# Top-k attention with a mixture of experts: shorter chains at five pairs of heads, six pairs' masks on another engine, and the first expert stage regrouped

## The chip, the cores and the metric

The kernel runs on one core of one Trainium2 chip. The metric is the device time of one execution in microseconds (us), the median of several runs.

## The reference, cut to what matters

```python
# q, k, v: (2, 8, 576, 64)
scores = matmul(q, k.T) / 8
kth    = 32nd largest of each row of 576 scores
scores = where(scores >= kth, scores, -1e9)
attn   = exp(scores - max); attn = attn / (sum(attn) + 1e-9)
x      = matmul(attn, v)                       # as (1152, 512), heads side by side
p      = probs / (sum(probs) + 1e-9)           # 4 experts
x      = sum over e of p[:, e] * (relu(x @ w1[e]) @ w2[e])        # 512 -> 1024 -> 512
h      = max(x @ m1, x @ m2, x @ m3); out = h @ m_out              # 512 -> 768 -> 512
```

The last four matrices come in as float64 and are made float32 on the chip.

## The kernel before, in words

**Attention** is cut into 36 pairs, numbered 1 to 36 here: 128 rows (one of nine tiles) of two heads. Each pair takes eight slots of an order written out in `attention()`; in a slot, every step that was put there with `at_slot` or `two` is emitted on its engine. The dictionaries `FIRST`, `TIGHT` and `LOOSE` say how many slots after the pair's first each step stands. Per head, DVE (VectorE) finds the 32 largest of 576 scores with four MAX8 (L434) and three MATCH_REPLACE8 (L436). Then the mask: a multiply by a comparison on DVE (L462, which also sums), or a comparison (L465) and a multiply (L466) on POOL (GpSimd) with the sum on ACT (L470), or three operations on ACT (ScalarE; L455 to L457, which also sum and take the exponent). `ON_POOL` and `ON_ACT` list by number from 0 which pair's head takes which. Then come transposes `psp` (L480, L485) and their copies `pt` (L483, L488), the guard on the sums `rs` (L493), the reciprocal (L499), its spread and transpose (`rb`, `psr`, `r`), the product with v `psv` (L522, L525), and the norm (L532), in which DVE multiplies `psv` by `r` and writes `x`. `split_x` makes a high and a low part of `x` for later matmuls.

**The experts** follow the tiles in stages. Stage 0 (tile 0 alone, `first_alone`, matmuls L751 and L766) and the stage of one other single tile (L788, L829) use unsplit float32 weights, called `whole`; the other stages use high and low parts of weights (`whi`, `wlo`, L268 and L274) and three matmuls for each product (L667 to L669). In stage 0 one expert's first layer came after the other's: e outside, the four 128-wide pieces a of the model dimension inside.

**The order of the expert work** is set while the program is built. `products()` is a generator of expert matmuls; after each slot the main loop advances it until its running count of PE time reaches a goal that grows by DVE's estimated time in that slot. If the next matmul's `x` is not made yet, what is left of that goal is dropped. So a piece of `x` that is made some slots earlier lets expert matmuls stand earlier in PE's queue. `x_ready` takes a pair's `x` once its slot `last` has passed; for the third pair of a tile, `READY` slots more.

**Weights** are loaded by SP's DMA queue: `raw` pieces, split on ACT and POOL, at most `W_AHEAD` (4) pieces ahead of use; `whole` pieces straight into the buffers of the split parts. The last 12 pieces of the program are of the final maximum over three products (`largest`), whose weights are converted from float64 in the slots from 306 on (`to_float32`).

**The end**: after pair 36 only expert and final matmuls are left. ACT copies each output tile out of PSUM (L947) and issues its DMA (L948).

Of the kernel before, what the change touches and what calls it, by code (L numbers as in the profile page):

```python
# [20 lines left out]
BEGIN, READY = 4, 4  # L21
# [17 lines left out]
FIRST = dict(stag=2, new=1, scores=-12, trans=11, pv=17, rec=16, lag=2, sum=4)  # L39
TIGHT = dict(stag=3, new=1, scores=-7, trans=9, pv=14, rec=12, lag=1, sum=0)  # L40
# [16 lines left out]
def kernel(  # L57
# [231 lines left out]
    def load_alone(n):  # L289
        while len(w_alone) < n:  # L290
            x, i, u = alone[len(w_alone)]
            n_ = len(w_alone)
            tag, bufs = ("raw", 4) if 10 <= n_ < 13 else (("hi", "lo")[n_ % 2 if n_ < 10 else (n_ - 13) % 2], 5)
            t = wp.tile([P, 1024], F32, tag=tag, bufs=bufs, name="whole")
            nc.sync.dma_start(out=t, in_=(w1, w2)[x == "b"][i // 2, 2 * (i % 2) + u])
            w_alone[x, i, u] = t.rearrange("p (a f) -> p a f", f=512 if x == "b" else 256)
# [251 lines left out]
    def attention():  # L548
# [3 lines left out]
        later = {}  # L552

        def options(n):
            return TIGHT if n in (HP - 1, 2 * HP - 1) else FIRST if n < 2 * HP else LOOSE

# [30 lines left out]
        for n, (c, hp, t) in enumerate(pairs):  # L587
# [7 lines left out]
            for j in range(2):  # L595
                b0 = s0 + o["stag"] * j
                two(b0 + o["scores"], pr.scores, j)
# [7 lines left out]
                late = MASK_LATE * pr.on_act[j]  # L605
                two(b0 + 7 + late, pr.mask, j, lag=o["sum"] if n < EARLY else 3)
                two(b0 + o["trans"] + late + (late > 0), pr.trans_p, j)
            two(s0 + o["stag"] + o["trans"], pr.trans_p, 2)
            at_slot(s0 + o["rec"] - 1, pr.guard)
            at_slot(s0 + o["rec"], pr.recip)  # L610
            at_slot(s0 + o["rec"] + 1, pr.spread)
            at_slot(s0 + o["pv"], pr.pv)
            two(s0 + o["rec"] + 2, pr.trans_r)
            end = max(o["pv"], o["rec"] + 2) + o["lag"]
            at_slot(s0 + end + 1, pr.norm)
            two(s0 + end + 2, pr.split_x)
        last = {}
        for n, p in enumerate(pairs):
            o = options(n)
            last[p[0:2]] = 8 * n + max(o["pv"], o["rec"] + 2) + 2 * o["lag"] + 2  # L620
        for n in range(13):
# [3 lines left out]
        while s <= end:  # L625
            todo = later.pop(s, [])
            i = 0
            while i < len(todo):
                f, a = todo[i]
                f(*a)  # L630
                todo += later.pop(s, [])
# [88 lines left out]
    def sums(t):  # L720
        if t < NTILE - MAXT:
            accs[t] = xp.tile([P, DM], F32, tag="acc", bufs=NTILE - MAXT, name="acc")
# [13 lines left out]
    def first_alone():  # L736
# [3 lines left out]
        for e in range(len(HALVES[0]) // 2):  # L740
# [248 lines left out]
    while advance():  # L989
        pass  # L990
# [65 lines left out]
```

## Time and profile before

| | us |
|---|---|
| median of 3 runs | 769.29 (769.08 to 770.25) |
| the profiled execution | 767.91 |
| its span | 766.0 |
| busy PE / DVE / ACT / POOL | 732.2 / 613.6 / 484.9 / 491.4 |

The profiled execution is 1.38 us under the median, and 1.9 us of it lie around its span. PE (TensorE) is busy for 96% of the span, but not for one reason throughout: a row of windows shows for each stretch which engine was full.

### The profile page before, as it was taken

What the parts mean: (1) busy time and instruction counts of PE and PEld (TensorE: products, weight loads), DVE (VectorE), ACT (ScalarE), POOL (GpSimd) and SP (SyncE); (2) the same over time, 40 slices, a digit from 0 to 9 for tenths busy, and PEclk for the clock granted to TensorE, in tenths of its full rate; (3) what the DMA queues carried; (4) which work ended last, traced back from release to release, by engine and by line L of the source; (5) the groups of instructions that cost most, each with busy time, mean ns of one, the idle gap of its engine ahead of it and who ended that gap; (6) DMA issues with size and microseconds to landing.
All of it is one profiled execution on the core that took longest, in us unless ns stands there. A gap on an engine that the chain in (4) does not pass through costs nothing.

```text
span 766.0 us, 13619 instructions
## 1 busy us (share of the span) xinstructions
PE 732.2 (96%) x4678; PEld 646.0 (84%) x4678; DVE 613.6 (80%) x1179; ACT 484.9 (63%) x1088; POOL 491.4 (64%) x419
## 2 busy tenths in 40 slices
PE   5888999999999999999999998999999999999997
PEld 3566668988899899888899877899998899999996
DVE  6999999989998999999999976899989544233341
ACT  4656767787977888878886754575655433343431
POOL 2648887979798887886976415777776632442520
PEclk9989999999999999999999999999999999999999
DMA  7572563566366444634543649878877442353511
GB/s 218 178 212 90 161 181 110 157 177 175 112 178 191 140 148 135 182 118 145 147 134 133 220 173 333 307 259 252 269 250 251 158 141 84 136 181 97 178 43 42
DMA packets 56053, 130.15 MB, mean 170 GB/s; under 512 B 9712, under 2 KB 23024, under 8 KB 55984
## 3 DMA queue, kind: packets, MB, share of 16 engines
q1 hardware_dynamic: 47632, 120.56, 50.6%
q10 hardware_dynamic: 8352, 8.72, 3.2%
q8 instruction: 37, 0.61, 0.3%
q14 instruction: 32, 0.26, 0.1%
HBM read 120.60 MB, written 8.65 MB: 169 GB/s over the span
## 4 chain that ended last, share of the span: by engine, by line
PE 65%; POOL 6%; issue 5%; ACT 4%; DVE 3%; DMA 2%; SPq 1%; ACTq 0%; POOLq 0%; DVEq 0%
PE ps L667 16%; PE ps L669 16%; PE ps L668 16%; POOL wlo L274 5%; PE psv L525 3%; PE pss L414 2%; PE psp L480 2%; PE pso L668 2%; PE pso L667 2%; PE pso L669 2%; DMA raw<-in_w_dram 2%; PE ps L829 1%; ACT whi L268 1%; DVE m L434 1%; PE psv L522 1%
## 5 line engine op out<-in xcount | busy, mean ns | idle before, releaser
L274 POOL TENSOR_TENSOR wlo<-raw,whi 128x512 fp32r<-128x512 f32 x228 | 303.8, 1360 | 128.8 <-ACT whi L268 123.9
L268 ACT ACTIVATE whi<-raw 128x1024 fp32r<-128x1024 f32 x148 | 154.1, 1060 | 38.7 <-PE ps L669 14.6
L667 PE MATMUL ps<-xl,whi 128*128 128x256 f32 (+1 forms) x520 | 158.9, 306 | 1.8 <-ACT pt L483 1.8
L668 PE MATMUL ps<-xh,whi 128*128 128x256 f32 (+1 forms) x520 | 156.6, 301 | 0.0
L669 PE MATMUL ps<-xh,wlo 128*128 128x256 f32 (+1 forms) x520 | 156.6, 301 | 0.0
L434 DVE MAX8 m<-work 128x8 f32<-128x576 f32 x216 | 154.8, 743 | 0.1
L436 DVE MATCH_REPLACE8 work<-m,work 128x576 f32<-128x576 f32 x144 | 106.5, 741 | 0.0
L274 DVE TENSOR_TENSOR wlo<-raw,whi 128x1024 fp32r<-128x1024 f32 x34 | 50.4, 1482 | 64.9 <-ACT whi L268 51.8
L667 PEld LDWEIGHTS ps<-xl,whi 128*128 128x128 f32 x520 | 97.8, 188 | 3.9 <-ACT pt L483 2.2
L668 PEld LDWEIGHTS ps<-xh,whi 128*128 128x128 f32 x520 | 97.7, 188 | 1.4 <-issue 0.5
L669 PEld LDWEIGHTS ps<-xh,wlo 128*128 128x128 f32 x520 | 97.6, 188 | 0.0
L245 POOL TENSOR_TENSOR narrow<-narrow,raw 128x256 int32<-128x256 int32 x48 | 47.4, 987 | 42.0 <-DVE narrow L242 12.8
L667 PE MATMUL ps<-wlo,h 128*128 128x512 f32 x160 | 64.0, 400 | 0.5 <-POOL wlo L274 0.5
L669 PE MATMUL ps<-whi,h 128*128 128x512 f32 x160 | 62.8, 393 | 0.5 <-POOL h L804 0.5
L668 PE MATMUL ps<-whi,h 128*128 128x512 f32 x160 | 62.8, 392 | 0.0
L421 ACT ACTIVATE s<-pss 128x288 f32<-128x288 f32 x144 | 51.8, 409 | 12.9 <-PE pss L409 12.7
L480 PE MATMUL psp<-ident,p 128*128 128x128 f32 x288 | 45.5, 283 | 11.3 <-POOL p L466 7.8
L434 DVE MAX8 m<-s 128x8 f32<-128x576 f32 x72 | 54.0, 750 | 2.5 <-ACT s L421 2.0
L436 DVE MATCH_REPLACE8 work<-m,s 128x576 f32<-128x576 f32 x72 | 53.3, 740 | 0.0
L480 PEld LDWEIGHTS psp<-ident,p 128*128 128x128 f32 x288 | 35.2, 145 | 20.0 <-POOL p L466 10.2
L483 ACT ACTIVATE pt<-psp 128x512 f32<-128x512 f32 x72 | 42.6, 592 | 11.3 <-PE psp L480 11.3
L667 PE MATMUL ps<-x2l,whi 128*128 128x384 f32 x144 | 48.7, 338 | 0.0
(116 smaller groups left out, 1661.2 us busy)
## 6 DMA issues: line engine op xcount, KB each, us to landing
raw<-in_w_dram SPq DMA_DIRECT2D x112, 512.0 KB, 4.0
raw<-narrow SPq DMA_DIRECT2D x36, 512.0 KB, 3.3
whole<-in_w_dram SPq DMA_DIRECT2D x32, 512.0 KB, 5.5
raw<-in_m_dram SPq DMA_DIRECT2D x36, 256.0 KB, 5.0
narrow<-narrow ACTq DMA_DIRECT2D x48, 128.0 KB, 4.2
kraw<-in_k_dram SPq DMA_DIRECT2D x16, 288.0 KB, 5.2
qraw<-in_q_dram SPq DMA_DIRECT2D x48, 64.0 KB, 3.9
raw<-in_mo_dram SPq DMA_DIRECT2D x12, 256.0 KB, 3.8
```

The costliest lines, as they stand in the source:

```text
L245: nc.gpsimd.tensor_tensor(out=out.bitcast(I32), in0=out.bitcast(I32), in1=last, op=ALU.add)
L268: nc.scalar.activation(out=hi, in_=raw, func=AF.Copy)
L274: on.tensor_tensor(out=lo[:, x], in0=raw[:, x], in1=hi[:, x].bitcast(F32), op=ALU.subtract)
L421: nc.scalar.activation(out=s[:, h, :], in_=halves[h][:, 0:SH], func=AF.Copy)
L434: nc.vector.max(m[:, 8 * r:8 * r + 8], src)
L436: nc.vector.match_replace(out=self.w[j], in_to_replace=m[:, 8 * r:8 * r + 8], in_values=src, imm_value=NEG)
L480: nc.tensor.transpose(ps[:, r * P:(r + 1) * P], self.p[:, part, part * TAIL + r * P:part * TAIL + (r + 1) * P], ident)
L483: return lambda: [nc.scalar.activation(out=d, in_=ps.rearrange("p (r n) -> p r n", r=NR), func=AF.Copy), self.did.add(("pt", part))]
L525: nc.tensor.matmul(ps[j * D:(j + 1) * D, cols], lhsT=vs[:, j * NR + r, :], rhs=self.pt[j][:, r, cols], start=False, stop=r == NR - 1)
L667: nc.tensor.matmul(ps, lhsT=lh, rhs=rl, start=first, stop=False)
L668: nc.tensor.matmul(ps, lhsT=lh, rhs=rh, start=False, stop=False)
L669: nc.tensor.matmul(ps, lhsT=ll, rhs=rh, start=False, stop=last)
```

## The change

1. Slots. Pairs 3 and 7 take a new `MIDDLE`, pairs 4 and 8 a new `TIGHT`, pair 12 a new `THIRD`. In these the second head's transposes, the reciprocal, the product with v and the norm stand fewer slots after the scores; in `TIGHT` and `THIRD` the norm is put between two top-k operations of its slot. `READY` goes from 4 to 1.
2. Masks. Of pairs 3 to 8 the first head's masks, and of pairs 3 and 7 the second's too, go from POOL to ACT: eight masks.
3. Stage 0. The loop over the pieces a is outside, both experts inside, so that each piece of `x` is used by both at once; the second expert's sums have PSUM banks from the start. Its whole weights: four in the `raw` buffers, ten in the buffers of the split parts, the last two as halves in the buffers of later sums (`acc2`), which are free then.
4. Loading. Three `raw` pieces of the next stage may be loaded right after stage 0's first layer. In the other single-tile stage `weight` looks two pieces further ahead. `begun` parts of stage 1 are followed by a flush of evictions.
5. The last output tile is copied in two halves, by ACT and DVE, each sent out by a queue of its own.
6. When no expert work is ready, the main loop leaves its inner loop.

```diff
-BEGIN, READY = 4, 4
+BEGIN, READY = 4, 1
-ON_POOL = ((0, 1, 2, 3, 4, 5, 6, 7), (0, 1, 2, 4, 5, 6))
+ON_POOL = ((0, 1), (0, 1, 4, 5))
-ON_ACT = (range(12, 36), ())
+ON_ACT = ((2, 3, 4, 5, 6, 7, *range(12, 36)), (2, 6))
-FIRST = dict(stag=2, new=1, scores=-12, trans=11, pv=17, rec=16, lag=2, sum=4)
-TIGHT = dict(stag=3, new=1, scores=-7, trans=9, pv=14, rec=12, lag=1, sum=0)
+FIRST = dict(stag=2, new=1, scores=-12, trans=11, pv=17, rec=16, lag=2, sum=4, late=1)
+MIDDLE = dict(stag=2, new=1, scores=-12, at=(11, 12), pv=14, rec=12, lag=1, sum=0, late=1)
+TIGHT = dict(stag=3, new=1, scores=-7, at=(10, 11), guard=11, rec=11, spread=12, pv=12, turn=12, norm=13, split=13, last=14, lag=0, lag_s=1, sum=0, late=1)
+THIRD = dict(stag=4, new=1, scores=-4, at=(11, 12), guard=12, rec=13, spread=13, pv=14, turn=14, norm=15, split=15, last=16, lag=0, lag_s=2, sum=0)
...
-        w_split_to(w_index[oldest or key] + W_AHEAD)
+        w_split_to(w_index[oldest or key] + W_AHEAD + 2 * whole(key))
...
-        for e in range(len(HALVES[0]) // 2):
-            banks = [po.tile([P, 512], F32, tag="o", name="psa") if not e else bank("psa") for _ in range(2)]
-            h = hp_.tile([P, 2, 512], F32, tag="h", bufs=4, name="hfull")
-            for a in range(KT):
-                while (0, a) not in x_ready:
-                    yield None
-                for y, ps in enumerate(banks):
+        for a in range(KT):
+            while (0, a) not in x_ready:
+                yield None
+            for e in range(len(HALVES[0]) // 2):
...
+                for y in range(2):
...
+        load_alone(len(alone))
         flush()
+        w_load_to(3)
...
-                    if not e:
-                        w_load_to(2 * y + u)
-                    else:
-                        w_split_to(2 * y + u + 1)
+                    if u:
+                        w_split_to(2 * e + y + 1)
...
-                nc.scalar.activation(out=ob, in_=ps, func=AF.Copy)
-                nc.scalar.dma_start(out=out[tiles[ti] * P:(tiles[ti] + 1) * P, :], in_=ob)
...
+                nc.scalar.activation(out=ob[:, 0:DM // 2], in_=ps[:, 0:DM // 2], func=AF.Copy)
+                nc.scalar.dma_start(out=rows[:, 0:DM // 2], in_=ob[:, 0:DM // 2])
+                nc.vector.tensor_copy(out=ob[:, DM // 2:], in_=ps[:, DM // 2:])
+                nc.sync.dma_start(out=rows[:, DM // 2:], in_=ob[:, DM // 2:])
```

On PE, from pair 4's product with v (`psv` with `v_last_112`) on; the scores `pss` belong to later pairs, `psa` is stage 0's first layer, `ps<-whole,hfull` its second. Before, from that product to pair 5's:

```order
L522 MATMUL psv<-pt_563,v_last_112 128x128
L525 MATMUL psv<-pt,vt 64x128 x8
L508 MATMUL psr<-ident,rb 128x128
L409 MATMUL pss<-kfull,qfull 128x288 x2
L480 MATMUL psp<-ident,p 128x128 x4
L751 MATMUL psa<-xfull,whole 128x128 x8
L480 MATMUL psp<-ident,p 128x128 x4
L485 MATMUL psp<-ident,p 128x128
L751 MATMUL psa<-xfull,whole 128x128 x20
```

Now:

```order
L530 MATMUL psv<-pt_580,v_last_112 128x128
L533 MATMUL psv<-pt,vt 64x128 x8
L516 MATMUL psr<-ident,rb 128x128
L417 MATMUL pss<-kfull,qfull 128x288 x2
L767 MATMUL psa<-xfull,whole 128x128 x2
L417 MATMUL pss<-kfull,qfull 128x288 x2
L767 MATMUL psa<-xfull,whole 128x128 x24
L782 MATMUL ps_713<-whole,hfull 128x512 x3
L488 MATMUL psp<-ident,p 128x128 x8
L493 MATMUL psp<-ident,p 128x128
L782 MATMUL ps_713<-whole,hfull 128x512 x4
```

Stage 0's first layer ends right behind pair 4's product, and seven matmuls of its second layer stand ahead of pair 5's.

On DVE, from the last mask of pair 4 (`m_440`) on. Before:

```order
L462 SCALAR_TENSOR_TENSOR p,rs<-s,m_440,p 128x576
L436 MATCH_REPLACE work<-m_539,s 128x576
L436 MATCH_REPLACE work<-m_499,work 128x576
L434 MAX m_539<-work 128x8
L434 MAX m_499<-work 128x8
L499 RECIPROCAL rr<-rs 128x2
L436 MATCH_REPLACE work<-m_539,work 128x576
L436 MATCH_REPLACE work<-m_499,work 128x576
L532 TENSOR_TENSOR xfull<-psv,r 128x128
```

Now:

```order
L470 SCALAR_TENSOR_TENSOR p,rs<-s,m_440,p 128x576
L444 MATCH_REPLACE work<-m_551,s 128x576
L444 MATCH_REPLACE work<-m_522,work 128x576
L507 RECIPROCAL rr<-rs 128x2
L442 MAX m_551<-work 128x8
L442 MAX m_522<-work 128x8
L444 MATCH_REPLACE work<-m_551,work 128x576
L540 TENSOR_TENSOR xfull<-psv,r 128x128
```

Before, the `xfull` row is pair 3's norm, and pair 4's comes later; now it is pair 4's own.

On PE, from the product with v of the last pair (`v_last_110`) on; L788, now L803, and L829, now L844, are the single-tile stage. Before:

```order
L522 MATMUL psv<-pt_6055,v_last_110 128x128
L525 MATMUL psv<-pt,vt 64x128 x8
L508 MATMUL psr<-ident,rb 128x128
L788 MATMUL ps_6099<-xfull,whole 128x128 x8
L788 MATMUL ps_6118<-xfull,whole 128x128 x8
L829 MATMUL ps_6004<-whole,hfull 128x512 x4
L788 MATMUL ps_6158<-xfull,whole 128x128 x8
L788 MATMUL ps_6179<-xfull,whole 128x128 x8
L829 MATMUL ps_6201<-whole,hfull 128x512 x4
L667 MATMUL ps_6234<-xl,whi 128x384
```

Now:

```order
L530 MATMUL psv<-pt_6090,v_last_110 128x128
L533 MATMUL psv<-pt,vt 64x128 x8
L516 MATMUL psr<-ident,rb 128x128
L844 MATMUL ps_5967<-whole,hfull 128x512 x3
L803 MATMUL ps_6145<-xfull,whole 128x128 x8
L803 MATMUL ps_6173<-xfull,whole 128x128 x8
L844 MATMUL ps_6192<-whole,hfull 128x512 x4
L679 MATMUL ps_6210<-xl,whi 128x384
```

Sixteen matmuls of the first layer and one of the second now stand ahead of the last product.

## Rows read from the trace of the kernel before

**Rows 1.** Windows: stretch, its length, busy us (instructions) by engine, PEclk, DMA share, GB/s.
```profile
40.00:60.00 20.00, 14.71 (x86) 10.87 (x85) 19.93 (x46) 11.58 (x36) 9.29 (x9) 0.83 0.66 182
60.00:80.00 20.00, 18.38 (x140) 16.29 (x139) 19.97 (x44) 13.13 (x36) 16.88 (x15) 0.91 0.38 118
80.00:100.00 20.00, 20.00 (x118) 12.18 (x117) 19.29 (x43) 16.78 (x45) 17.24 (x14) 1.00 0.59 174
...
160.00:450.00 290.00, 284.26 (x2181) 255.81 (x2180) 274.36 (x582) 231.29 (x549) 219.78 (x191) 1.00 0.50 150
...
600.00:766.00 166.00, 162.16 (x871) 152.69 (x869) 58.70 (x77) 60.25 (x85) 58.76 (x40) 0.99 0.34 118
```

**Rows 2.** Waits of DVE, 160 to 450 us: total us, times, longest us.
```profile
DVE h L811 <- ACT h L809: 6.8, 7, 1.5
DVE xt L532 <- POOL wlo L274: 3.4, 3, 1.8
DVE xt L532 <- ACT r L510: 1.7, 2, 1.2
DVE xfull L532 <- ACT r L510: 1.3, 2, 1.1
DVE rr L499 <- ACT rs L493: 1.0, 2, 0.7
DVE acc L733 <- PE ps L669: 0.9, 1, 0.9
DVE xt L532 <- issue: 0.3, 1, 0.3
```

**Rows 3.** Timeline of PE at the end of attention: start us, us, engine, line, [idle before <-releaser].
```profile
451.54 0.49 PE L522 MATMUL psv<-pt,v_last 128*128 128x128 f32 x2 [0.99 <-ACT pt L488]
...
453.15 3.74 PE L788 MATMUL ps<-xfull,whole 128*128 128x128 f32 x32
456.72 1.45 PE L829 MATMUL ps<-whole,hfull 128*128 128x512 f32 x3
```

**Rows 4.** Waits of PE, 0 to 160 us, the largest.
```profile
PE psp L480 <- POOL p L466: 7.8, 5, 2.1
```

**Rows 5.** Timeline of PE, first stage's matmuls at two clock levels.
```profile
45.71 3.78 PE L751 MATMUL psa<-xfull,whole 128*128 128x128 f32 x16
...
64.37 4.63 PE L751 MATMUL psa<-xfull,whole 128*128 128x128 f32 x40
```

**Rows 6.** Timeline of PE, the two waits behind attention.
```profile
465.38 1.96 PE L829 MATMUL ps<-whole,hfull 128*128 128x512 f32 x4 [1.49 <-DMA whole<-in_w_dram]
467.97 1.95 PE L829 MATMUL ps<-whole,hfull 128*128 128x512 f32 x4 [0.63 <-ACT narrow L235]
```

**Rows 7.** Timeline of ACT, the last output tile.
```profile
762.20 0.60 ACT L947 ACTIVATE ob<-pso 128x512 f32<-128x512 f32 x1 [3.61 <-PE pso L669]
```

**Rows 8.** Timeline of DVE around the last mask of pair 4.
```profile
49.58 0.82 DVE L462 SCALAR_TENSOR_TENSOR p<-s,m,p 128x576 f32<-128x576 f32 x1
...
50.39 0.74 DVE L436 MATCH_REPLACE8 work<-m,s 128x576 f32<-128x576 f32 x1
...
51.78 1.41 DVE L434 MAX8 m<-work 128x8 f32<-128x576 f32 x2
53.11 0.15 DVE L499 RECIPROCAL rr<-rs 128x2 f32<-128x2 f32 x1
```

**Rows 9.** Timeline of DVE around the last pair's mask and norm.
```profile
449.48 0.08 DVE L462 DVE_READ_ACCUMULATOR p<-s,m,p 128x1 f32 x1
...
453.73 0.29 DVE L532 TENSOR_TENSOR xt<-psv,r 128x128 f32<-128x128 f32 x1 [3.67 <-ACT r L510]
```

**Rows 10.** Timeline of PE, two matmuls of 128x256 in a row.
```profile
114.69 0.28 PE L667 MATMUL ps<-xl,whi 128*128 128x256 f32 x1
114.81 0.28 PE L668 MATMUL ps<-xh,whi 128*128 128x256 f32 x1
```

**Rows 11.** Lines by form: masks, sums, table load: busy us, mean ns, idle before.
```profile
L465 POOL TENSOR_SCALAR s<-s,m 128x576 f32<-128x576 f32 x14 | 24.1, 1722 | 33.8 <-ACT s L421 13.8 <-DVE m L434 11.1 <-PE pss L409 6.1
...
L466 POOL TENSOR_TENSOR p<-p,s 128x576 f32<-128x576 f32 x14 | 19.7, 1406 | 1.2
L455 ACT ACTIVATE s<-s,m 128x576 f32<-128x576 f32 x24 | 18.9, 787 | 0.0
L457 ACT ACTIVATE p<-s,nb 128x576 f32<-128x576 f32 x24 | 18.6, 777 | 0.8
...
L470 ACT ACTIVATE s<-p 128x576 f32<-128x576 f32 x14 | 9.5, 679 | 11.6 <-POOL p L466 11.6
...
L122 ACT ACT_TABLE_LOAD x1 | 1.3, 1283 | 1.4 <-PEq L1035 1.4
```

More of the change, by code (lines that the diff above doesn't have):

```diff
@@ L292, in load_alone @@
             n_ = len(w_alone)
[L293 to L296, printed above, removed]
+            src, f = (w1, w2)[x == "b"][i // 2, 2 * (i % 2) + u], 512 if x == "b" else 256
+            if n_ >= 14:
+                halves = [xp.tile([P, DM], F32, tag="acc2", bufs=4, name="whole") for _ in range(2)]
+                for y, t in enumerate(halves):
+                    nc.sync.dma_start(out=t, in_=src[:, y * DM:(y + 1) * DM])
+                w_alone[x, i, u] = halves
+                continue
+            t = wp.tile([P, 1024], F32, tag="raw" if n_ < 4 else ("hi", "lo")[n_ % 2], bufs=4 if n_ < 4 else 5, name="whole")
+            nc.sync.dma_start(out=t, in_=src)
+            w_alone[x, i, u] = t.rearrange("p (a f) -> p a f", f=f) if x == "a" else [t[:, y * DM:(y + 1) * DM] for y in range(2)]
     kraw, kT, vt, qraw, qT = {}, {}, {}, {}, {}
@@ L551, in attention @@
         prs = {}
-        later = {}
+        later, between = {}, {}
         def options(n):
-            return TIGHT if n in (HP - 1, 2 * HP - 1) else FIRST if n < 2 * HP else LOOSE
+            return TIGHT if n in (HP - 1, 2 * HP - 1) else MIDDLE if n in (HP - 2, 2 * HP - 2) else FIRST if n < 2 * HP else THIRD if n == 3 * HP - 1 else LOOSE
         def at_slot(s, f, *a):
@@ L596, in attention @@
                 b0 = s0 + o["stag"] * j
-                two(b0 + o["scores"], pr.scores, j)
+                two(b0 + o["scores"], pr.scores, j, lag=o.get("lag_s", o["lag"]))
                 for i in range(7):
@@ L619, in attention @@
             o = options(n)
-            last[p[0:2]] = 8 * n + max(o["pv"], o["rec"] + 2) + 2 * o["lag"] + 2
-        for n in range(13):
+            last[p[0:2]] = 8 * n + o.get("last", max(o["pv"], o["rec"] + 2) + 2 * o["lag"] + 2)
+        for n in range(len(alone)):
             at_slot(ALONE_FROM + ALONE_STEP * n, load_alone, n + 1)
@@ L630, in attention @@
                 f(*a)
+                todo[i + 1:i + 1] = between.pop(s, [])
                 todo += later.pop(s, [])
@@ L721, in sums @@
         if t < NTILE - MAXT:
-            accs[t] = xp.tile([P, DM], F32, tag="acc", bufs=NTILE - MAXT, name="acc")
+            accs[t] = xp.tile([P, DM], F32, tag="acc" if t < 2 else "acc2", bufs=2 if t < 2 else NTILE - MAXT - 2, name="acc")
         else:
@@ L765, in first_alone @@
                         pe(4 * DM)
-                        nc.tensor.matmul(ps, lhsT=h[:, y, (2 * u + f) * P:(2 * u + f + 1) * P], rhs=w[:, f, :],
+                        nc.tensor.matmul(ps, lhsT=h[:, y, (2 * u + f) * P:(2 * u + f + 1) * P], rhs=w[f],
                                          start=y == u == f == 0, stop=y == u == f == 1)
                         yield True
-                    if not e:
-                        w_load_to(2 * y + u)
-                    else:
-                        w_split_to(2 * y + u + 1)
+                    if u:
+                        w_split_to(2 * e + y + 1)
+                    if e and not y and not u:
+                        tick()
             later(gated(ps, 0, e, not e, False))
-        flush()
     def experts():
```

36 lines of the change are left out of this document (25 added, 11 removed).

## The prediction

> **What bounds the kernel now.** I read the windows first, to see which engine is full where [rows 1]. From 160 to 450 us DVE is busy for 274.36 of 290 us and PE for 284.26; from 600 to 766 PE is busy for 162.16 of 166 and DVE for 58.70. So there are two stages. The attention's top-k operations on DVE pace the first, because the order of the program ties PE's expert work to them; behind the last product with v, which starts at 451.54 [rows 3], PE runs through what is left and nothing else counts. Hence the rule by which I sum: the time is the moment of the last product, plus the PE work and the PE waits behind it. Work that moves from behind that product to ahead of it is gained, if PE has room ahead of it and DVE isn't made to wait for it.
>
> The waits came next. DVE waits in 160 to 450 for 15.4 us in all, the sum of the seven rows, nearly half of it for ACT's `h`, which follows expert matmuls, 6.8 us [rows 2]. Before 160 PE waits most for masks made on POOL, 7.8 us in five waits [rows 4]. That does not lengthen the kernel by itself, since DVE is busy for 19.93 and 19.97 of 20 us in 40 to 60 and 60 to 80 [rows 1]; but PE's idle time there, 5.29 and 1.62 us, is room in which expert work could stand.
>
> **Work moved ahead of the last product.** The order of PE shows 16 first-layer matmuls and one second-layer matmul of the single-tile stage moved ahead of it, and the same instructions in total. The 16 took from 453.15 to 456.72, 3.57 us [rows 3]. A second-layer matmul makes two records; four records took 1.96 us [rows 6], at most 0.98 for one, with a tail that the next one hides; I take 0.9. That is **-4.5 us**, and it is the large term. Its bounds are 0 (the lead is handed back, a rival below) and -4.5.
>
> Where is the room? The lead is made early. 22 more `psa` matmuls stand ahead of pair 4's product (38 for 16); ahead of pair 5's, 20 more `psa` (64 for 44) and seven of the second layer (7 for 0). One `psa` matmul is two records: 0.23 us at the full clock (40 records in 4.63) and 0.47 at the low one (16 in 3.78) [rows 5]. So PE has 20 x 0.23 + 7 x 0.9 = 10.9 us more ahead of pair 5's product. From 40 to 80 it was idle for 6.9 us, and its granted clock was 0.83 and 0.91 [rows 1]; at 1.00 the same work would take 14.71 x 0.17 + 18.38 x 0.09 = 4.2 us less. Room of 11.1 us against 10.9: it fits, with nothing to spare, if the clock goes up. In rows 1 it does so where PE is fuller: 1.00 where it is busy for 20.00 of 20 us, 0.83 where for 14.71. The Trainium skill (TensorE: Matmul & The Clock Gate, What's actually happening) says the same, that the throttled state is the default and recent activity releases it; by that rule the denser stretch runs at the full level, and these rows agree. Later the lead shrinks: ahead of pair 13's product it is 12 matmuls of 128x256 and 24 of 128x512, some 7.2 us by 0.12 for a 256-wide one, the distance of two starts [rows 10], and twice that for a 512-wide one, and 4.5 at the last.
>
> **Masks.** Eight masks leave POOL, 1.72 + 1.41 us each, 25 us in all, with their sums on ACT of 0.68; ACT takes 0.79 + 0.78 and a small one instead of the sum and of a plain exponent [rows 11], net at most 1 us a mask, 8 in all. From the last MAX to the masked scores the way shortens by about 1 us. ACT is busy for 11.58 to 16.78 of 20 us there [rows 1], so these lie beside DVE's work; without that cover they would cost up to 8. The value is **0**: they make room for PE, counted above. The Trainium skill (ScalarE: Activation LUTs, What ACT_TABLE_LOAD costs) has a rule against this: each switch to a different set of functions costs a load and a drain. By it each mask would add two loads of 1.28 us to its chain. The trace has one load in the whole span, though 24 masks already run on ACT between copies and exponents [rows 11]; hence 0.
>
> **Shorter chains on DVE.** In the new order pair 4's norm stands five top-k operations and the reciprocal behind its last mask. By pair 4's rows before that is 1.4 + 1.3 + 0.1 + 0.7 = 3.5 us of DVE work: from 50.39 to 51.78, on to 53.11, the reciprocal, and 0.74 less its overlap [rows 8]. The chain that the norm waits for ran without cover once, at the last pair: from the end of the mask at 449.56 to the norm at 453.73, 4.2 us [rows 9]. Here six `psa` matmuls, 1.4 us, lie in PE's queue ahead of the product; 1.0 of it fits in the wait for `pt`, 0.99 there [rows 3], so the chain is 4.6 and DVE stands for 1.1. At pair 8 four operations and the reciprocal give 2.9 us of cover, and nine 128x256 matmuls of 0.12 make the chain 4.3: 1.4. Together **+2.5 us**, bounds 0 (the transposes run sooner than at the last pair, since the first head's `psp` is out earlier) and +5 (each chain also meets a queue on ACT, which now makes masks). Pair 12's norm has more cover; 0. Queued behind the waiting norm on DVE are the next pairs' top-k operations, and that is why the wait counts in full. That `READY` lets stage 1 start sooner is in the lead above.
>
> **DVE's waits in 160 to 450.** PE has 7.2 - 4.5 = 2.7 us less work in that stretch than before, since the lead shrinks. DVE's waits for `h` are waits for PE, so part of this comes back: not quite half, **-1.2**, bounds -3 and +2 (expert work that is placed afresh can meet other top-k operations).
>
> **Weights.** The order of SP has four more `whole` loads of the later single-tile stage ahead of the five conversion loads, so the waits of PE at 465.38 (1.49 us, for a `whole` load) and 467.97 (0.63 us) [rows 6] lose their reason, in part: **-1.2** of 2.1, bounds 0 and -2.1. The first `raw` loads of stage 1 move ahead of two early k and q loads on SP's queue; those are needed some 20 us later, so 0. The halves in `acc2` wait for no buffer; 0. The flush after `begun` parts moves evictions, not matmuls; 0.
>
> **End.** The last copy took 0.60 us [rows 7]; two halves side by side take somewhat more than half: **-0.2**, bounds 0 and -0.5; the DMAs behind it are as long.
>
> **Sum.** -4.5 + 2.5 - 1.2 - 1.2 - 0.2 = -4.6 on the profiled 767.91: 763.3. The median of the runs lies 1.38 above the profiled time, so 764.7. The bounds of the terms give -4.5 + 0 - 3 - 2.1 - 0.5 = -10.1 and -4.5 + 5 + 2 = +2.5. A measurement can tell about 0.2%, 1.5 us: faster is under 767.8, slower over 770.8.
>
> **Rivals.** (A) *DVE's waits go.* The expert work of 160 to 450 stands earlier, and half of the 15.4 us [rows 2] vanishes: -7.7 in place of -1.2, 758.2. For it: the largest row is of PE's lateness. Against: PE is as full as before there. Chance 0.06. (B) *The lead is handed back.* PE was idle for only 5.7 us in 160 to 450, and the 17 matmuls delay scores and products there as much as they save behind: 4.5 lost, 769.2. For it: DVE's own slack there is 15.6 us and already all waits. Against: the early room of 11 us. Chance 0.12. (C) *Slower by the clock.* If the 48 `psa` matmuls between pair 3's and pair 5's products run at the 1.2 GHz level, each costs 0.24 more [rows 5], 11.5 us. Ten top-k operations, about 7.2 us, stand between pair 5's reciprocal and its norm, the chain there takes 3.7 [rows 9], so 3.5 is covered and DVE stands for 8.0: 772.7. It decides against this change from about 40 of the 48 on. For it: at 45.71 these very matmuls ran at that level. Against: the stretch is denser now. Chance 0.10. (D) *A table load at every mask.* 2 x 1.28 in the chains of pairs 4 and 8, 5.1 us: 769.8. Against: one load with 24 masks [rows 11]. Chance 0.02.
>
> **Numbers.** My forecast has 0.70, and nearly all of it lies under 767.8. Faster: 0.70 + 0.06 = 0.76. Same: B and D, 0.14. Slower: C, 0.10. The range from 759.0 to 769.5 holds my forecast and B, and leaves out A, C and D, 0.18.
>
> **What the next profile would show.** Right: the last product with v at about 450 us, and the second-layer rows (three matmuls) right behind it; a granted clock near 1.00 from 50 to 80; no POOL masks beyond six; DVE waits of about 1 us at the norms of pairs 4 and 8; no wait for `whole` after attention. Wrong: a last product at 455 (B), a clock under 0.9 from 50 to 70 with DVE waiting for scores or `r` (C), or more than one table load (D).

## The result and the profile after

The changed kernel takes 773.17 us (median of 4 runs, 772.57 to 773.95), the kernel before 769.18 beside it: a ratio of 1.0052, interval 1.0032 to 1.0072. It is 4.0 us slower where 4.6 us faster was forecast, and outside the range. The profiled execution took 773.95 us, its span 772.2.

The prediction summed by one rule: the moment of the last product with v, plus what lies behind it. First the timeline of PE at that product, after (before: 451.54, [rows 3]).

```profile
464.62 0.49 PE L530 MATMUL psv<-pt,v_last 128*128 128x128 f32 x2 [0.99 <-ACT pt L496]
...
466.24 2.74 PE L844 MATMUL ps<-whole,hfull 128*128 128x512 f32 x6
```

The last product comes at 464.62, 13.1 us later. Behind it lie 772.2 - 464.62 = 307.6 us, where 766.0 - 451.54 = 314.5 lay: 6.9 less. The second-layer matmuls of the single-tile stage now stand right behind it, as forecast. PE's waits from 445 us to the end, after, hold one row, and that is the product's own; both waits of [rows 6] are gone.

```profile
PE psv L530 <- ACT pt L496: 1.0, 1, 1.0
```

So the part behind the last product gained more than forecast, and everything was lost ahead of it. Where it was lost first is in PE's timelines, at the products of pairs 8 and 9, before and then after:

```profile
97.05 0.49 PE L522 MATMUL psv<-pt,v_last 128*128 128x128 f32 x2
...
111.75 0.49 PE L522 MATMUL psv<-pt,v_last 128*128 128x128 f32 x2
```

```profile
95.60 0.63 PE L530 MATMUL psv<-pt,v_last 128*128 128x128 f32 x2
...
120.61 0.38 PE L530 MATMUL psv<-pt,v_last 128*128 128x128 f32 x2
```

Pair 8's product came 1.5 us sooner than before, pair 9's 8.9 us later. The windows between the two, before and then after, with the columns of [rows 1]:

```profile
97.05:111.75 14.70, 13.01 (x90) 10.14 (x90) 13.93 (x29) 10.70 (x27) 14.62 (x13) 1.00 0.72 194
```

```profile
95.60:120.61 25.01, 21.77 (x152) 19.39 (x152) 19.27 (x41) 13.99 (x32) 15.03 (x13) 0.95 0.33 92
```

Of 14.7 us DVE was busy for 13.9, of 25.0 it is for 19.3. The windows of [rows 1], after:

```profile
40.00:60.00 20.00, 19.20 (x152) 16.03 (x152) 19.47 (x45) 12.68 (x39) 2.37 (x4) 1.00 0.85 261
60.00:80.00 20.00, 20.00 (x99) 12.00 (x99) 19.97 (x45) 16.68 (x42) 14.18 (x12) 1.00 0.55 172
80.00:100.00 20.00, 16.11 (x109) 12.24 (x109) 15.28 (x36) 15.54 (x43) 13.78 (x13) 0.83 0.38 103
...
160.00:450.00 290.00, 278.69 (x2109) 249.28 (x2110) 269.48 (x573) 227.98 (x541) 219.64 (x192) 0.99 0.51 149
```

From 40 to 80 us PE is fuller (19.20 and 20.00 us where 14.71 and 18.38 were), and its granted clock is 1.00 where it was 0.83 and 0.91: the room that the prediction counted was there and was used, and DVE lost only 0.5 us of busy time (19.47 and 19.97 for 19.93 and 19.97). From 80 to 100 PE runs dry (16.11), the clock falls to 0.83, and DVE, which was busy for 19.29 us there, drops to 15.28. From 160 to 450 DVE has 4.9 us less busy time than before, and PE 5.6 less: both stand more often. (The window is the same, but the work in it begins some 9 us later.) The waits of DVE from 30 to 175 us, the two largest (all rows: 14.2 us, before 3.5):

```profile
DVE h L826 <- ACT h L824: 9.0, 4, 4.0
DVE xt L540 <- ACT r L518: 3.4, 1, 3.4
```

And from 160 to 450, the three largest rows, which answer to [rows 2] (all rows: 20.5 us, before 15.4):

```profile
DVE h L826 <- ACT h L824: 8.2, 6, 4.0
DVE xt L540 <- POOL kT L340: 4.2, 1, 4.2
DVE xt L540 <- ACT r L518: 3.4, 3, 2.4
```

DVE's waits for `h` in 30 to 175 went from 0.2 to 9.0 us. The longest of them, 4.01 us at 167.72, stands in both lists; from 175 to 450 the waits for `h` are 4.2 us, where 6.6 were. But the waits from 160 to 450 grew by 5.1 us in all, where 1.2 less had been forecast. Where the early ones lie is in the timeline of DVE after; the first row is the end of pair 8's mask, the second its norm, the third stage 0's last sum, the others `h`.

```profile
92.42 0.08 DVE L470 DVE_READ_ACCUMULATOR p<-s,m,p 128x1 f32 x1
...
98.79 0.29 DVE L540 TENSOR_TENSOR xt<-psv,r 128x128 f32<-128x128 f32 x1 [3.45 <-ACT r L518]
...
101.05 0.73 DVE L745 SCALAR_TENSOR_TENSOR acc<-ps,gate,acc 128x512 f32<-128x512 f32 x1
...
113.39 0.69 DVE L826 SCALAR_TENSOR_TENSOR h<-ps,h 128x512 fp32r<-128x512 f32 x1 [1.89 <-ACT h L824]
...
129.03 0.69 DVE L826 SCALAR_TENSOR_TENSOR h<-ps,h 128x512 fp32r<-128x512 f32 x1 [2.44 <-ACT h L824]
...
167.72 0.69 DVE L826 SCALAR_TENSOR_TENSOR h<-ps,h 128x512 fp32r<-128x512 f32 x1 [4.01 <-ACT h L824]
```

DVE stands 3.45 us at pair 8's norm, then 1.89, 2.44 and 4.01 us for parts of `h`. These follow matmuls that stand in PE's queue. PE's timeline at the same place:

```profile
89.95 0.65 PE L488 MATMUL psp<-ident,p 128*128 128x128 f32 x4 [1.59 <-ACT p L465]
92.56 1.11 PE L488 MATMUL psp<-ident,p 128*128 128x128 f32 x4 [1.95 <-DVE p L470]
...
93.89 0.41 PE L680 MATMUL ps<-xh,whi 128*128 128x256 f32 x1
94.11 0.41 PE L681 MATMUL ps<-xh,wlo 128*128 128x256 f32 x1
...
96.16 1.98 PE L533 MATMUL psv<-pt,vt 128*64 128x128 f32 x16
...
101.84 0.39 PE L679 MATMUL ps<-xl,whi 128*128 128x256 f32 x1 [1.84 <-DVE acc L745]
```

PE had no expert work left at 88 to 93 us: it waited for the two masks of pair 8, 1.59 and 1.95 us. Then 128x256 matmuls start 0.22 apart, where 0.12 was the distance at 2.4 GHz [rows 10]: this is the 1.2 GHz level, and pair 8's product with v takes 1.98 us where 1.09 is the time at the full level. At 101.84 it waits for a sum that DVE made only after the norm.

### The profile page after: what moved, and what is told of

Read it like the earlier page. It is cut to its first block, busy times and chain, and to the rows that moved or that the text cites. A ratio compares the mean times of both kernels' runs of the same rounds, so it can differ in the third digit from the quotient of the medians.

```text
span 772.2 us, 13598 instructions
## 1 busy us (share of the span) xinstructions
PE 734.9 (95%) x4678; PEld 645.6 (84%) x4678; DVE 613.4 (79%) x1180; ACT 487.2 (63%) x1096; POOL 465.6 (60%) x403
## 4 chain that ended last, share of the span: by engine, by line
PE 61%; DVE 20%; ACT 11%; issue 4%; POOL 3%; DMA 1%; ACTq 0%; POOLq 0%; DVEq 0%
PE ps L679 14%; PE ps L681 14%; PE ps L680 14%; DVE m L442 8%; DVE work L444 7%; ACT whi L270 3%; PE psv L533 3%; DVE p L470 2%; POOL wlo L276 2%; PE ps L803 2%; PE ps L844 2%; PE pso L681 2%; PE pso L680 2%; PE pso L679 2%; PE psa L767 2%
## 5 line engine op out<-in xcount | busy, mean ns | idle before, releaser
L276 POOL TENSOR_TENSOR wlo<-raw,whi 128x512 fp32r<-128x512 f32 x228 | 308.4, 1380 | 124.7 <-ACT whi L270 123.9
L276 DVE TENSOR_TENSOR wlo<-raw,whi 128x1024 fp32r<-128x1024 f32 x34 | 52.5, 1544 | 58.0 <-ACT whi L270 46.7
L488 PE MATMUL psp<-ident,p 128*128 128x128 f32 x288 | 45.0, 282 | 11.1 <-DVE p L470 4.5
```

The lines of the kernel that those rows point to most:

```text
L276: on.tensor_tensor(out=lo[:, x], in0=raw[:, x], in1=hi[:, x].bitcast(F32), op=ALU.subtract)
L488: nc.tensor.transpose(ps[:, r * P:(r + 1) * P], self.p[:, part, part * TAIL + r * P:part * TAIL + (r + 1) * P], ident)
```

## The experiments

The first theory, H, was read from these rows: a hole ahead of pair 8's product, a fall of the clock, and a pack of expert work behind it (15.7 us by the order between pair 8's and pair 9's product, where by the records of the trace before some 9 us stood, an estimate), so that PE is late on its own account and DVE waits for `h`. The rivals: the norm's place (N), the masks on ScalarE (M), pair 12's lead (T). Last products and waits are those of one profiled execution each, and executions of one kernel differ by up to some 6 us; so where the medians tell another difference, it is given too.

**Pair 8's norm later.** `TIGHT` for pair 8 with `norm=15, split=15, last=16` in place of 13, 13, 14.

> One edit to the changed kernel: pair 8's norm stands two slots, four top-k operations, later on DVE; the order on PE is the same. Theory H (a hole: PE runs out of expert work ahead of pair 8's product, its clock falls, and the order then packs 15.7 us of expert work ahead of pair 9's product, so that PE is late on its own account): DVE's wait of 3.45 us at that norm shrinks below 1, but PE only gets back its wait of 1.84 us for the sum behind the norm, and DVE waits for h instead: 771 to 773. Rival N (the norm's place alone makes the loss, and the later waits follow from it): the last product comes 6 us or more sooner, 767 or less.

772.77 us; the last product came at 463.38, 1.2 us sooner. The wait of 3.45 is gone and DVE's waits of 30 to 175 us are 11.9 in place of 14.2, 9.9 of it for `h`. N falls, and H's numbers hold.

**Masks back on GpSimd.**

```diff
-ON_POOL = ((0, 1), (0, 1, 4, 5))
+ON_POOL = ((0, 1, 2, 3, 4, 5, 6, 7), (0, 1, 2, 4, 5, 6))
-ON_ACT = ((2, 3, 4, 5, 6, 7, *range(12, 36)), (2, 6))
+ON_ACT = (range(12, 36), ())
```

> One edit to the changed kernel: all masks of the first eight pairs are made where the kernel before made them (eight go from ScalarE back to GpSimd). The order on PE is the same. Theory H: the masks are beside the cause; the chain at pair 8 gets about 1 us longer and the hole with it, 772 to 776. Rival M (the masks on ScalarE delay its copies and splits): most of the 13 us by which the last product came later goes, 765 or less.

789.07 us: 16 slower than the changed kernel, far beyond what was expected. M falls, and H's range is far exceeded: with the masks on GpSimd the short slots leave DVE without cover. Its reciprocal, placed a few operations behind its mask, waited 9.97 us for a sum (timeline of DVE):

```profile
98.02 0.17 DVE L507 RECIPROCAL rr<-rs 128x2 f32<-128x2 f32 x1 [9.97 <-ACT rs L501]
```

**Pair 8 in its old slots**, `TIGHT8 = dict(stag=3, new=1, scores=-7, trans=9, pv=14, rec=12, lag=1, sum=0, late=0)`.

> One edit to the changed kernel: pair 8 takes the old TIGHT slots (transposes, product and norm two to three slots later). On PE 31.5 us of expert work then stand ahead of its product instead of 29.4, and 13.6 instead of 15.7 between it and pair 9's; from there on the order is the same, the lead at the last product too. Theory H: a smaller hole and a smaller pack, and DVE has cover for the norm: the last product 3 to 6 us sooner, 767 to 770. Rival N: the norm's wait is gone here too, 767 or less. Rival M: no change, 772.5 to 774.

770.77 us, last product 459.76, 4.9 us sooner. It lies 0.8 us above H's range for the time and within that for the product; N falls. The profiled execution is the shortest of ten (769.06), and that of the changed kernel the longest of four; the medians differ by 2.4 us. This execution settles one thing more: its granted clock is 1.00 throughout (the mean too is 1.000), and its last product is still 8.2 us later than the kernel before's. The largest row of DVE's waits from 30 to 175 us is that of the changed kernel:

```profile
DVE h L827 <- ACT h L825: 9.0, 4, 4.0
```

So these waits for `h` need no fall of the clock.

**Pair 12 in its old slots**, `THIRD` out of `options`.

> One edit to the changed kernel: pair 12 takes LOOSE again. From its product on, the order of PE has the same expert work ahead of each product as the kernel before, so the 4.5 us of lead at the last product are gone. Theory H, as far as the loss up to pair 9 is concerned: that stays (pair 9's product at about 120). Of the time behind: 6.9 us less are packed ahead of pair 12's product, the waits of 4.0 and 2.4 us for h go, the last product comes 7 us sooner, the rest behind it is 4.5 longer: 770 to 772. Rival T (pair 12's lead makes the greater part of the loss): the last product comes 11 us sooner or more, 767 or less.

769.54 us. The last product (timeline of PE):

```profile
456.10 0.49 PE L530 MATMUL psv<-pt,v_last 128*128 128x128 f32 x2 [0.99 <-ACT pt L496]
```

It comes 8.5 us sooner than in the changed kernel, and 311.6 us lie behind it, 4.0 more. So pair 12's short chain buys 4.0 us of lead at the end and costs 8.5 ahead of it. (By the medians it costs 3.6 in all, and so some 7.6 ahead of it.) H holds in kind, half a microsecond under its range; T would have had 767 or less.

**The tail alone**, in the kernel before: `w_split_to(... + W_AHEAD + 2 * whole(key))` and the last tile in two halves.

> Two parts of the change alone, in the kernel before: the weights of the later single-tile stage are asked for two pieces further ahead, and the last output tile is copied in two halves. The order on PE is that of the kernel before. Both the prediction and theory H expect the same: PE's waits of 1.49 and 0.63 us behind attention go, and 0.2 us at the end: 1.4 to 2.4 us less, 766.5 to 767.5. Rival: the waits move to later loads on the same queue, no change.

766.31 us, ratio 0.9968 (0.9957 to 0.9979): 2.6 us less (1.6 to 3.3), a little beyond the range; the rival falls. The term was forecast as 1.4.

**The masks alone**, in the kernel before, with the two lines of the second run the other way round and `late=1` in `FIRST` (0 for pairs 3 and 7).

> One part of the change alone, in the kernel before: the eight masks on ScalarE, in the old slots (pairs 3 and 7 begin their masks at the same slot as before, the others one slot later). The order on PE is that of the kernel before, but for 0.4 us at pair 5. Theory H: masks are worth nothing by themselves, since DVE paces here: 768 to 770. Rival M: ScalarE's queue delays its copies and splits, 772 or more. Rival G (GpSimd's 25 us were a hidden bound, as the run with masks put back at 789 suggests): 766 or less.

766.71 us, ratio 0.9971 (0.9961 to 0.9981): 2.2 us less. The forecast and H had put this at nothing; it lies between H's range and rival G's. The profiled execution, one of the longest of eleven (767.96), doesn't have the gain: its last product comes 1.1 us sooner (450.48), and 315.6 us lie behind it where 314.5 lay. Where the 2.2 us arise these runs don't show.

**Stage 0 with the experts outside again**, the old loop in `first_alone`.

> One edit to the changed kernel: in stage 0 the experts are outside again and the pieces inside. On PE 3.5 us less expert work stand ahead of pair 5's product, and 4.0 us in place of 0.9 between pair 7's and pair 8's products where PE ran dry; from pair 8's product on the order is the same. Theory H: the hole ahead of pair 8's product closes in part and PE's clock stays up: the wait of 3.45 us at pair 8's norm shrinks, the last product 2 to 5 us sooner: 769 to 771.5. Rival S (stage 0 regrouped is a gain by itself, since it gives PE work early): slower than the changed kernel, over 774.

771.64 us, last product 2.4 us sooner. That is H's figure for the product and 0.1 us above its range for the time; S falls. The regrouped loop is no gain in this order.

**Pairs 8 and 12 both old.**

> Two edits to the changed kernel: pair 8 takes the old TIGHT slots and pair 12 the old LOOSE ones. If the two losses add (4.9 us at the last product for pair 8, and 8.5 less 4.5 of lead for pair 12), then 771.9 to 773.2 less 8.4 at best: 765 to 767, under the kernel before. If pair 8's gain is taken back by waits that pair 12's pack hid, 768 to 769.

768.55 us, ratio 0.9991 (0.9982 to 1.0). The losses don't add: with pair 12 old, taking pair 8 back moved the last product by only 0.4 us (456.10 to 455.67). It was the second of the two cases expected.

**Masks and tail together**, in the kernel before.

> The kernel before with three parts of the change: the eight masks on ScalarE in the old slots, the weights of the later single-tile stage two pieces further ahead, and the last output tile in two halves. The two gains were measured alone as 2.6 and 2.2 us. They lie at different places (behind and ahead of the last product), so they should add: 763.5 to 765.0. If they overlap, 766 to 767.

763.84 us, ratio 0.9938 (0.9924 to 0.9952). The two gains add. The last product is where the kernel before had it, less 1.2 us, and DVE's waits of 30 to 175 us are the four small rows below. This version is 4.9 us faster than the kernel before and 9.3 faster than the changed one.

```profile
450.36 0.49 PE L523 MATMUL psv<-pt,v_last 128*128 128x128 f32 x2 [0.99 <-ACT pt L489]
```

```profile
DVE xt L533 <- POOL wlo L275: 1.8, 1, 1.8
DVE acc L738 <- ACT acc L736: 1.6, 1, 1.6
DVE xt L533 <- ACT r L511: 0.4, 1, 0.4
DVE h L816 <- ACT h L814: 0.3, 1, 0.3
```

**A filler for the clock**: in the changed kernel, ahead of each half of pair 8's transposes,

```diff
+FILL = 6
...
+            if self.n == 2 * HP - 1 and part < 2:
+                for _ in range(FILL):
+                    nc.tensor.matmul(ps, lhsT=kT[0, 0][:, 0, 0:P], rhs=kT[0, 0][:, 0, 0:512], start=True, stop=True)
```

> The changed kernel, with twelve matmuls of 128x512 whose results are thrown away (2.8 us, six ahead of each half of pair 8's transposes, where PE waited 1.59 and 1.95 us with nothing to do). The rest of the order is the same. Theory H, its part on the clock: the granted clock stays at 1.00 from 80 to 100, the product of pair 8 and what stands ahead of it run at the full level, about 2 us sooner, and DVE's wait at the norm falls from 3.45 to about 1.5: pair 9's product 1 to 2 us sooner, the time 771 to 773. If the clock is the main part of the early loss, 769 or less. If the fall of the clock costs nothing because PE is late only by what it is given, 773 to 774.

772.53 us, last product 464.65, where the changed kernel had 464.62. The windows from 80 to 110 us, DVE's norm of pair 8, and DVE's largest wait from 30 to 175 us; then the window from 100 to 110 of the changed kernel:

```profile
80.00:100.00 20.00, 17.07 (x128) 12.71 (x127) 17.84 (x41) 16.87 (x46) 13.89 (x13) 1.00 0.40 112
100.00:110.00 10.00, 10.00 (x74) 10.00 (x73) 8.27 (x17) 3.62 (x8) 2.90 (x3) 0.83 0.33 89
```

```profile
96.13 0.29 DVE L544 TENSOR_TENSOR xt<-psv,r 128x128 f32<-128x128 f32 x1 [0.89 <-ACT r L522]
```

```profile
DVE h L830 <- ACT h L828: 10.1, 4, 4.0
```

```profile
100.00:110.00 10.00, 8.16 (x69) 8.16 (x70) 10.00 (x21) 4.09 (x11) 1.80 (x3) 1.00 0.39 106
```

From 80 to 100 us the clock is back at 1.00, and the wait at the norm is 0.89 in place of 3.45. Pair 9's product comes 1.1 us sooner (119.50), as H had it. That gain is still there at pair 15's product (200.96 for 203.31) and gone at pair 16's (217.02 for 216.58). But the fall of the clock didn't go, it moved: to 0.83 from 100 to 110, and to 0.76 from 210 to 215, where the changed kernel has 1.00 both times. So in these two executions the low clock at pair 8's product didn't set the last product; what the clock costs altogether the run doesn't show. The time is within H's range, but only 0.6 us under the changed kernel's. Of its seven executions the three with a mean granted clock of 1.0 took 770.07, 770.78 and 773.35 us, and the changed kernel's four, at 0.992 to 0.996, 772.57 to 773.95: a share of up to some 3 us for the clock is not excluded.

**PE paced at 0.9 in stage 1**, `SHARE = (1.0, 0.9, 1.0)`: in the order, less expert work ahead of pairs 9 to 13, and nearly the same lead at the end.

> One edit to the changed kernel: in stage 1 the order gives PE 0.9 of DVE's estimated time instead of 1.0. Ahead of pair 9's, 10's, 11's and 13's products stand 43.7, 50.7, 59.0 and 74.3 us of expert work in place of 45.1, 54.8, 64.6 and 78.4, and ahead of the last 264.8 in place of 265.7. Theory H, its part on packing (DVE waits for h because more is packed than PE can do beside it): the waits of 2.4 and 4.0 us for h go, the last product comes 4 to 7 us sooner and 0.9 us is added behind it: 767 to 770. If packing isn't the cause, the last product stays and the time is 773 to 774.5.

770.20 us, last product 461.11. Between 30 and 175 us the waits for `h` are gone (6.5 us of other waits stay, for 14.2 in all); DVE's largest wait from 175 to 450 shows where they went (4.2 us for `h` in the changed kernel):

```profile
DVE h L826 <- ACT h L824: 14.8, 7, 5.2
```

The last product comes 3.5 us sooner, just short of H's 4 to 7, and the time is 0.2 us above its range: part of the price is gone, and the rest has moved to a later place. A lead that is built later is paid for later.

**Stage 1 let in later**: `READY = 8` in the run with the old pairs 8 and 12.

> The run with the old pairs 8 and 12 (768.55) and one edit more: READY is 8 in place of 1, so that stage 0 and stage 1 may use the third pair of a tile seven slots later. All chains, masks, loads and the loops stay as changed. Ahead of pair 9's to 12's products stand 36.8, 47.9, 57.6 and 65.9 us of expert work in place of 45.1, 54.8, 64.6 and 67.3 (33.6, 43.7, 53.4 and 63.2 in the kernel before); from pair 13's on, the order is that of the kernel before, in all three. Theory L (an early lead is paid for in waits of DVE for h and brings nothing once it is gone at pair 13): the 5.0 us of waits for h between 100 and 160 go, the last product comes 3 to 5 us sooner, 764 to 766. Rival C (the shorter chains or the moved loads themselves make the early loss): the last product stays within 1.5 us, 767.5 to 769.5.

769.59 us, last product 455.91, as without the edit (455.67). Theory L in this form fell: with the start of stage 1 put off, pair 9's product came 5.3 us sooner, but pair 13's no sooner (170.55 against 170.31). DVE still waited 6.4 us for `h` between 30 and 180. Rival C has the last product right, and the time to 0.1 us.

**Three parts undone one at a time**, in the run with the old pairs 8 and 12: the flush at the end of stage 0 kept; all of stage 0 as before; pair 4 in its old slots.

> The run with the old pairs 8 and 12 (768.55), with the flush at the end of stage 0 put back as in the kernel before: the second expert's sum is issued on DVE at once, so that stage 1's second begun part need not wait for its PSUM bank. The order on PE is the same. Theory F (PE's waits of 0.7 to 3.6 us for that sum start the chain of late work): PE's wait for the sum goes, DVE's waits for h between 100 and 135 shrink from 5.0 below 2.5, the last product 2 us sooner or more: 765 to 767. Rival C (the sum's wait is only one of several on PE, and the next takes its place): within 1 us, 767.8 to 769.3.

> The run with the old pairs 8 and 12 (768.55), with all of stage 0 as in the kernel before: its loop, its whole weights' places and loads, and the order of the next stage's raw loads. The shorter chains of pairs 3, 4 and 7, READY of 1, the masks on ScalarE, the flush after begun parts and the tail stay changed. Theory W (the moved loads and the regrouped stage 0 make the early loss of 4 to 5 us): the last product at 452 or before, 764 to 766. Rival C (the chains in the new slots make it): the last product stays at 455 or so, 767.5 to 769.5.

> The run with the old pairs 8 and 12 (768.55), with pair 4 in the old TIGHT slots too. Theory C (the short chains make the early loss, each by a wait of DVE at its norm): DVE's waits of 0.8 and 1.5 us at the norms of pairs 3 and 4 go, the last product 1 to 2.5 us sooner: 766 to 767.7. Theory W: no change, 768 to 769.3.

768.00, 767.78 and 772.09 us, with last products at 455.80, 454.34 and 458.70 (455.67 without). The first is rival C's number, F falls. The second is within C's range too, with its product 1.3 us sooner; W falls. The third is worse by 3.5, where theory C had 0.9 to 2.6 better and W no change. Undoing one part of a packed order makes the order anew and moves the waits; these runs could not tell the parts apart. So the last three went the other way and added one part to the version without the loss.

> The best version so far (masks on ScalarE and the tail, 763.84), with the new TIGHT slots for pair 4 alone. The expert work ahead of each product is the same at every pair. Theory C (each short chain costs DVE a wait at its norm): 1 to 2 us slower, 764.8 to 766. If the waits come only from the packed order, no change: 763.3 to 764.5.

> The best version so far, with the new TIGHT slots for pair 8 alone. From pair 9's product on the order of PE is the same; 2.6 us of expert work move from ahead of pair 8's product to behind it. Theory C: a wait of 1.4 to 3.5 us at the norm, 765 to 767.5. If the waits come only from the packed order: 763.3 to 764.5.

> The best version so far, with the new MIDDLE slots for pairs 3 and 7 alone. That makes the early lead: 43.7 us of expert work ahead of pair 9's product in place of 33.6, 63.2 in place of 53.4 ahead of pair 11's, and none at pair 13's. Pairs 4 and 8 keep their old, covered norms. Theory P (a lead is paid for by DVE's waits for h, and brings nothing once it is gone): waits for h of 3 us or more between 100 and 140, 2 to 5 us slower, 766 to 769. Theory C: no change or a gain, 763 to 764.5.

| added to masks and tail (763.84) | median | last product | behind it | DVE's waits, 30 to 175 |
|---|---|---|---|---|
| nothing | 763.84 | 450.36 | 311.4 | 4.1 |
| pair 4 in the new slots | 764.05 | 450.55 | 311.5 | 4.2 |
| pair 8 in the new slots | 766.25 | 452.84 | 311.5 | 5.8 |
| pairs 3 and 7 in the new slots | 770.30 | 459.65 | 311.5 | 12.4 |
| (the changed kernel) | 773.17 | 464.62 | 307.6 | 14.2 |

The median is over all executions, the other columns are of the profiled one. For pair 4 theory C falls, for pair 8 it holds: DVE waits 1.31 us at that norm. The runs of the fourth row spread from 766.8 to 773.0, and its profile was the longest of them, so its 6.5 us are a middle, above theory P's range. It is the largest price all the same. DVE doesn't wait at the norms of pairs 3 and 7; what their slots do is to let expert work in earlier, 43.7 us of it ahead of pair 9's product in place of 33.6. How that cost DVE time in this execution is to be seen in the window from 60 to 80 us, and in DVE's and PE's timelines at pair 5 (the last DVE row is pair 9's norm):

```profile
60.00:80.00 20.00, 20.00 (x146) 17.43 (x147) 16.37 (x37) 13.71 (x40) 8.58 (x8) 0.93 0.25 86
```

```profile
73.70 0.74 DVE L438 MATCH_REPLACE8 work<-m,work 128x576 f32<-128x576 f32 x1
78.08 0.29 DVE L534 TENSOR_TENSOR xt<-psv,r 128x128 f32<-128x128 f32 x1 [3.63 <-ACT r L512]
...
127.20 0.29 DVE L534 TENSOR_TENSOR xt<-psv,r 128x128 f32<-128x128 f32 x1 [3.57 <-ACT r L512]
```

```profile
54.52 0.79 PE L524 MATMUL psv<-pt,v_last 128*128 128x128 f32 x2 [1.92 <-ACT pt L490]
55.24 1.98 PE L527 MATMUL psv<-pt,vt 128*64 128x128 f32 x16
...
59.77 8.04 PE L757 MATMUL psa<-xfull,whole 128*128 128x128 f32 x56
...
68.63 4.18 PE L757 MATMUL psa<-xfull,whole 128*128 128x128 f32 x36
72.65 0.39 PE L524 MATMUL psv<-pt,v_last 128*128 128x128 f32 x2
...
75.16 0.33 PE L510 MATMUL psr<-ident,rb 128*128 128x128 f32 x1
```

PE is busy for 20.00 of 20 us, DVE for 16.37. Between pair 4's product at 54.52 and pair 5's at 72.65 stand 92 records of `psa`, 46 matmuls; then come scores, then the transpose `psr` at 75.16. Its copy `r` stands in ACT's queue behind two evictions of stage 0 and a split of k:

```profile
75.57 1.08 ACT L761 ACTIVATE hfull<-psa 128x512 f32<-128x512 f32 x2
76.53 1.26 ACT L333 ACTIVATE kT<-kraw 128x576 fp32r<-128x576 f32 x2
...
77.76 0.29 ACT L512 ACTIVATE r<-psr 128x128 f32<-128x128 f32 x1
```

DVE's norm waits until 78.08, 3.63 us. Two things make PE late here. One is the pack: the version without these slots has 26 `psa` matmuls at this place, and 20 more are 4.7 us at the full clock. The other is the clock. Ahead of pair 4's product PE had nothing to do for 1.92 us, and that product took 1.98 us where 1.09 is full pace; the granted clock is 0.50 from 54 to 62 us and 1.00 from 64 on. By the distances between starts in this timeline, the low clock took some 3.9 us (an estimate), as much as DVE's wait. Ahead of the wait at pair 9's norm lies another such stretch: matmuls of 128x512 start 0.43 us apart there, and 0.23 at the same place in the changed kernel. The clock alone doesn't do it either: in the version without these slots it is 0.79 and 0.87 from 50 to 60 and 60 to 70, and DVE doesn't wait at pair 5. How much of the 6.5 us is the pack's without a low clock was not tried. Theory P had looked for the waits at `h`; they are 2.1 us there and 7.2 at the norms of pairs 5 and 9.

## Why the prediction was wrong, step by step

- **The rule of the sum** held, and better than hoped: in the eleven runs that keep the order of the kernel before from pair 13 on, with the new tail, 311.4 to 311.8 us lie behind the last product, and in the seven with pair 12's lead 307.5 to 308.0.
- **Work moved ahead of the last product, -4.5**: as a price of the part behind it, right; it is 311.6 - 307.6 = 4.0. As a gain it was wrong. The condition in the rule, that PE has room and DVE isn't made to wait, failed. Pair 12's lead put the last product 8.5 us later for those 4.0 (7.6 by the medians).
- **"Room of 11.1 us against 10.9: it fits, with nothing to spare"**: this is the step that failed. The room was there: PE did the 10.9 us at the full clock, and DVE lost 0.5 us up to 80. But the balance ended at pair 5's product, and from there on the rule's condition, that DVE isn't made to wait, was taken as met, but for the waits of the short chains themselves. Between pair 8's and pair 9's products the order packs some 7 us more expert work than before, where PE had been busy for 13.01 of 14.70 us: room of 1.7 for 7. The two products now lie 25.0 us apart, and DVE's waits from 30 to 175 us went from 3.5 to 14.2. PE's time over a stretch says nothing of when DVE needs what stands behind the expert work in the same queue: each piece ahead of a transpose or a product that is longer than its cover stops DVE. Of what pair 9's product is late by, 8.0 us in the run without pair 12's lead, 3.4 come back while the lead melts. The rest doesn't: from pair 13 on, its products keep a distance of 4.6 us from those of the kernel before, 170.79 against 166.21 there and 456.10 against 451.54 at the end.
- **"Later the lead shrinks"** was read and hardly used. The lead of 11.5 us ahead of pair 9's product is zero at pair 13's without pair 12's change. What was paid for it is lost, since by the rule of the sum only the lead at the last product counts.
- **DVE's waits in 160 to 450, -1.2**: wrong in sign. The rows of waits there add up to 20.5 us for 15.4, and DVE's busy time fell from 274.36 to 269.48.
- **Shorter chains, +2.5**: pair 4 was forecast at 1.1 and costs 0.2 alone, pair 8 at 1.4 and costs 2.4 alone. Pair 8's wait was 1.31 at its norm in that run and 3.45 in the changed kernel. The chain borrowed from the last pair was about right, but its stretch at a fallen clock was not in it.
- **Masks, 0**: they gain 2.2 us alone, and the changed kernel without them is 16 us slower. Taken as cover for PE only, they were undersold. The trace has one table load after, too, so rival D did not come about.
- **Weights and end, -1.4**: measured 2.6. Both waits of [rows 6] went whole.
- **The bounds.** The lead's term was given bounds of 0 and -4.5, but the upper end of the sum took it at -4.5. With 0 it is +7, and the measured +4.0 lies inside.
- **The rivals.** B, the lead handed back, was the mechanism, but its price was bounded by the lead itself, 4.5. The cost of a lead isn't bounded by what it returns. C gave the right time, 772.7, by luck: it looked for the low clock from 50 to 70 us, where the changed kernel's clock was 1.00. Its mechanism, `psa` matmuls at the 1.2 GHz level ahead of pair 5's product and DVE waiting behind them, did come in the profiled execution with the new slots of pairs 3 and 7 alone. The Trainium skill (TensorE: Matmul & The Clock Gate, What's actually happening) has the clock follow recent activity; the trace agrees at both places, 1.00 with 19.20 of 20 us busy and 0.83 with 16.11.

What stays open: the last product of the run with the old pairs 8 and 12 is 4 to 5 us later than without its new slots and stage 0 (455.67 for 451.54 and 450.36), and that was not split between stage 0's new loop and loads and the chains. The chains of pairs 3 and 7 alone cost that much or more, but in the one profile of them with a low clock beside them, and the parts overlap. Stage 0's new code with all the old chains was not tried. Nor was the clock's share measured: the run with pair 8 old shows 9.0 us of waits for `h` with no fall of it, and no profile has the changed kernel with the clock up throughout.

## What to carry to other kernels

In this kernel PE's queue is filled by an order made ahead of time. Work moved forward in it counted only by how much was still ahead at the end of the stage that DVE paces; in between it delayed what stood behind it. So weigh a lead against the cover of each consumer behind it, one by one and up to the place where the lead is gone, and not against the idle time of one stretch. And price a bundle of edits part by part by adding each to the old kernel: here two parts gave 4.9 us together, and the other parts took 9.3 back. A profile shows one execution: before its waits are read as a price, see where that execution stands among all, and what its granted clock was.

## What was not expected

The last output tile was split so that ACT and DVE would copy a half each. They ran one after the other. Timelines of ACT and of DVE, after:

```profile
768.62 0.38 ACT L968 ACTIVATE ob<-pso 128x256 f32<-128x256 f32 x1 [3.60 <-PE pso L681]
...
769.04 0.42 DVE L970 COPY ob<-pso 128x256 f32<-128x256 f32 x1 [10.57 <-ACT ob L968]
```

DVE's half starts at 769.04, and the trace gives ACT's copy as what released it, though the two read and write different columns. Both halves are of one tile; that this is the reason is likely and not shown. From the start of the copy to the end of the span it is 772.2 - 768.62 = 3.6 us, where it was 766.0 - 762.20 = 3.8 [rows 7]. The 0.2 us forecast came, but not from two copies side by side.
